# Windowed attention and a squared-ReLU layer on one core: loads without a gate from tile 9 on, scores of tiles 12 on two steps sooner

## The chip, the cores and the metric

The kernel runs on one core of a Trainium2 chip. A core has five engines that work side by side, each through its own list of instructions in order: TensorE multiplies matrices (in the profile PE, and PEld for its loading of weights), VectorE (DVE) and ScalarE (ACT) work on elements, GpSimd (POOL) here only starts loads, and SyncE (SP) starts the other DMA transfers. All transfers run on the core's 16 DMA engines. An engine waits for another through semaphores, and a transfer tells by a semaphore that it has landed. The metric is the device time of the program in microseconds (us); less is better.

## The reference

The inputs are q, k and v of 4 batches, 8 heads, 768 positions and 64 values per head, and the weights w_in (512 x 2048) and w_out (2048 x 512), all float32. First comes attention, in which a position sees the first 8 positions of its batch and the 96 positions up to itself, with a bias that falls with the distance by a slope of its own for each head; then, for each of the 3072 rows of 512 values, a layer with a squared ReLU:

```python
scores = scale * np.matmul(q, k.transpose(0, 1, 3, 2))
is_global = pos[None, :] < int(n_global)            # 8
is_local = (rel >= 0) & (rel < int(n_local))        # 96
keep = is_global | is_local
dist = np.where(is_global & ~is_local, float(n_local), np.abs(rel).astype(np.float32))
scores = scores + -slopes[:, None, None] * dist
scores = np.where(keep, scores, -1000000000.0)
a = softmax(scores)                                 # over the last axis
attn = np.matmul(a, v)
x = attn.transpose(0, 2, 1, 3).reshape(B * S, H * D)
h = x @ w_in
r = np.maximum(h, 0.0)
out = (r * r) @ w_out
```

## The kernel before

**Tiles and blocks.** The 3072 rows are 24 *tiles* of 128 positions, six per batch; two tiles are a *block* of the layer, so there are 12 blocks. Since the window is 96 long, a tile's queries need the keys of their own tile and of the one before; the 8 global keys are copied into that one's place.

**What happens to a tile j.** (1) *Load*: POOL starts three transfers, q, k and v (`load_tile`, the DMA at L200), which change float32 to bfloat16 on the way. q and k go into a slot of the ring `qk_ring`; tiles from 6 on share three slots, so tile j takes the slot of tile j - 3. v has a buffer for each tile. (2) *Turn*: the values of a head must lie along the partitions for the products. For the first six tiles TensorE transposes q and k; from tile 6 on one DMA transposition, started by SP (L407, `qkT<-qk`), does it. I call it the turn of tile j. When it has landed, the slot is free. (3) *Scores*: 16 small products per tile on TensorE (L463, `sc<-qkT`), 8 for the first tile of a batch. (4) ScalarE takes the exponential (L509, `esc<-sc`), VectorE multiplies it by a table of the bias and the mask (L534, `at<-esc`). (5) *Values*: TensorE multiplies with v in two halves of four heads (L576, `po<-v,at`), VectorE divides by the sum (L603, L604), which gives the tile's x. (6) *Move of x*: from tile 6 on a second DMA transposition on SP (L663, `xT<-x`) turns x for the layer.

**What happens to a block.** For each of eight steps s, TensorE makes an *up group*, eight products of 256 columns with w_in (L689, `hT<-xT,win`); ScalarE takes the ReLU (L710), VectorE squares it (L722, `hs<-hr`), and TensorE makes two *down pairs*, two products of 512 columns each with w_out (L759, `acc<-wout,hs`), one for each tile of the block. After the eighth step ScalarE or VectorE copies each tile's sum (L315, L317, `o<-acc`), and SP stores it (L794).

**What sets the order.** The order is not written out by hand. The program describes each piece of work as an operation with its engine, a cost, the operations that it needs and a due time, the *key*; the class `Plan` then goes through them, always taking the operation with the least start plus a hundredth of its key, and the result is the order of instructions on each engine. The key of a tile's work comes from its *base*, counted in steps of the layer, eight to a block:

```python
need = 8 * (j // 2)
base = need - LEADS.get(j, LEAD) + 4 * (j % 2)      # LEAD = 12
```

`LEADS` is a table of exceptions. Besides, scores of tile j may not be planned ahead of a certain up group (end of `order1`), which uses LEAD alone.

**The gate.** A load is issued by POOL in program order. For tiles from 8 on the plan puts an operation ahead of it, the *gate*: VectorE writes zeros into one column of the slot (L357). The load overwrites it, so POOL has to wait until VectorE has come to that place in its own list. The gate needs the end of the slot's last turn, the data of the tile before, and comes after the move of x of tile j - 3 was issued. Its `emit` is:

```python
nc.vector.memset(qk_ring[slot(j)][:, :, :1], 0.0)
```

**The queues.** POOL's list is loads alone, in the order of tiles after the start-up. SP's list holds turns, moves of x and stores, in the plan's order; each waits at the head of the queue for its own data, and what stands behind it waits with it. In the kernel before, SP's list runs, with the tile's number: turn 8, x 7, turn 9, x 8, two stores, turn 10, x 9, turn 11, x 10, two stores, turn 12, x 11, turn 13, x 12, two stores, turn 14, and so on.

Of the kernel before, what the change touches and what calls it, by code (L numbers as in the profile page):

```python
# [104 lines left out]
def kernel(  # L105
# [17 lines left out]
    NT = B * TPB  # L123
# [17 lines left out]
    NFIRST = 4  # L141
# [3 lines left out]
    NQ, NKT = 3, 2 * TPB  # L145
# [29 lines left out]
    pbt = const([P, 2, P], FP32, "pbt")  # L175
    pbw = const([P, 2, P], FP32, "pbw")
    plan = Plan()
    LEADS = {6: 10, 7: 11}
    NHS = 14
    NWARM = 8  # L180
    NLATE, NO = 2, 4
# [9 lines left out]
    def slot(j):  # L191

        return j if j < NFIRST + 2 else NFIRST + 2 + j % NQ
# [34 lines left out]
    def load_tile(j):  # L228
        load_part(0, j)
        load_part(1, j)  # L230
        load_v(j)
# [111 lines left out]
    for j in range(NT):  # L343
        b, t = divmod(j, TPB)
        first = t == 0
        need = 8 * (j // 2)
        base = need - LEADS.get(j, LEAD) + 4 * (j % 2)


        if j in late:  # L350
            def emit_load(e, j=j):
                load_tile(j)
            gate = None
            if j >= NFIRST + 2 + NQ - 1:

                def emit_gate(e, j=j):
                    nc.vector.memset(qk_ring[slot(j)][:, :, :1], 0.0)  # L357

                gate = plan.op(
                    ("gate", j), {"DVE": 0.07}, emit_gate, deps=qk_users[slot(j)] + [ld, xT_sp.get(j - 3)],  # L360
                    key=base - 9,
                )
            ld = plan.op(
                ("load", j), {"POOLQ": 2.6}, emit_load,
                deps=qk_users[slot(j)] + [ones[j], gate], key=base, ready=issue[0],
            )
            qk_users[slot(j)] = []
            ld = plan.op(("data", j), {"DMAQ": 2.7}, None, deps=[ld])
            land["q", j] = land["k", j] = land["v", j] = ld
# [360 lines left out]
    for o in plan.ops:  # L730
        if o["name"][0] == "sc":
            j = o["name"][1]
# [113 lines left out]
```

## Time and profile before

| | |
|---|---|
| time, median of 4 runs | 213.78 us (213.58 to 214.06) |
| time of the profiled execution | 214.06 us |
| its span, first to last instruction | 212.3 us |
| TensorE busy | 205.0 us, 97% of the span, at full granted clock |
| VectorE, ScalarE, POOL busy | 139.7, 119.9, 73.8 us |
| loads: q, k, v, from issue to landing, median | 4.6, 5.1, 5.7 us |
| turns (x18) and moves of x (x18), from issue to landing, median | 3.5 and 3.6 us |
| stores, from issue to landing, median | 2.2 us |

The profile is of one execution. Its times count from the start of the span. A line of the timeline gives start, length, engine, source line, operation, what is written from what, how many in a row, and in brackets how long the engine was idle before, and what ended that. A line of the chain of work gives start, length and what; the chain goes back from the last instruction, at each step to what released it. A line of the waits gives who waited at which line for whom, the sum in us, how often, and the longest. A transfer's line on POOL or SP shows its issue alone; when it landed is a separate figure. The products of TensorE are pipelined, so their lengths overlap; the step from one start to the next tells the pace.

### The profile page before, as it was taken

Reading aid. Unit: us, or ns where it says so; the run is one execution under the profiler, and the core shown is the slowest. Engines: PE = TensorE matmul, PEld = TensorE weight load, DVE = VectorE, ACT = ScalarE, POOL = GpSimd, SP = SyncE. Lnnn points to the kernel's source line nnn. Section 1 sums busy time; section 2 is a strip of 40 time slices with the busy share of each in tenths; the row PEclk is TensorE's granted clock in tenths of the full one; section 3 lists DMA queues with packets and bytes.
Section 4 is the critical chain, followed back from the end, with each engine's and each line's share of the span. In section 5 each row is a group of like instructions: output and inputs, shape, how many; then the busy total and the mean of one; then the engine's idle time right before and its main releaser. Section 6 shows DMA issues by size and latency. Waiting matters only on the chain.

```text
span 212.3 us, 5014 instructions
## 1 busy us (share of the span) xinstructions
PE 205.0 (97%) x1976; PEld 141.2 (67%) x1976; DVE 139.7 (66%) x377; ACT 119.9 (56%) x223; POOL 73.8 (35%) x91
## 2 busy tenths in 40 slices
PE   7999999999999999989989999999999999999994
PEld 3778777656766767757656767666767667666773
DVE  7789878524876966755757677575677587464530
ACT  6897478215664573753845854753845754743531
POOL 8998665440404413404404404314134310000000
PEclk9999999999999999999999999999999999999999
DMA  9999999999799999799999699998999894210202
GB/s 133 148 176 185 185 192 199 172 190 140 180 105 119 182 114 124 141 150 87 153 130 101 107 182 93 119 185 96 164 141 99 115 183 80 88 36 3 99 2 99
DMA packets 113703, 27.59 MB, mean 130 GB/s; under 512 B 104336, under 2 KB 110736, under 8 KB 113680
## 3 DMA queue, kind: packets, MB, share of 16 engines
q0 software_dynamic: 79200, 13.37, 82.6%
q1 hardware_dynamic: 34480, 13.90, 33.2%
q8 instruction: 15, 0.25, 0.5%
q14 instruction: 8, 0.07, 0.1%
HBM read 27.26 MB, written 6.29 MB: 158 GB/s over the span
## 4 chain that ended last, share of the span: by engine, by line
PE 78%; DMA 10%; POOL 7%; ACT 1%; issue 1%; SPq 0%; POOLq 0%; ACTq 0%
PE acc L759 36%; PE hT L689 33%; DMA qkT<-qk 6%; PE sc L463 5%; DMA win<-in_moe_w_in_dram 4%; POOL qk L200 4%; PE po L576 4%; POOL v L200 2%; POOL win L200 1%; ACT o L315 1%; ACT esc L509 1%; SPq L794 0%; POOL wout L200 0%; PE trx L639 0%; ACT hr L710 0%
## 5 line engine op out<-in xcount | busy, mean ns | idle before, releaser
L759 PE MATMUL acc<-wout,hs 128*128 128x512 bf16 (+1 forms) x400 | 99.0, 371 | 0.0
L689 PE MATMUL hT<-xT,win 128*128 128x256 bf16 x768 | 98.3, 273 | 0.6 <-DMA win<-in_moe_w_in_dram 0.4
L710 ACT ACTIVATE hr<-hT 128x512 f32<-128x512 f32 x96 | 57.7, 601 | 72.5 <-PE hT L689 69.5
L689 PEld LDWEIGHTS <-win 128*128 128x128 bf16 x768 | 73.9, 98 | 25.7 <-DMA win<-in_moe_w_in_dram 1.6
L722 DVE TENSOR_TENSOR hs<-hr 128x512 bf16<-128x512 f32 x96 | 65.7, 688 | 32.5 <-ACT hr L710 31.4
L200 POOL DMA_DIRECT2D qk<-in_q_dram x23 | 20.6, 896 | 90.2 <-DVE qk L357 56.1
L759 PEld LDWEIGHTS <-hs 128*128 128x128 bf16 x400 | 35.7, 98 | 23.7
L509 ACT ACTIVATE esc<-sc 128x512 bf16<-128x512 f32 x78 | 43.6, 608 | 5.1 <-PE sc L463 5.1
L534 DVE TENSOR_TENSOR at<-esc,E 128x512 bf16<-128x512 bf16 x78 | 32.2, 422 | 11.2 <-ACT esc L509 9.9
L200 POOL DMA_DIRECT2D v<-in_v_dram x24 | 21.7, 904 | 1.4 <-DMA win<-in_moe_w_in_dram 1.0
L604 DVE TENSOR_TENSOR x<-po,rs 128x256 bf16<-128x256 f32 x48 | 20.4, 425 | 1.7
L200 POOL DMA_DIRECT2D qk<-in_k_dram x23 | 20.5, 899 | 0.5 <-DMA win<-in_moe_w_in_dram 0.5
L576 PEld LDWEIGHTS <-at 128*128 128x128 bf16 x352 | 16.1, 98 | 4.6 <-ACT at L509 0.8
L576 PE MATMUL po<-v,at 128*128 128x65 bf16 x352 | 17.8, 193 | 0.5 <-ACT at L509 0.3
L463 PEld LDWEIGHTS <-qkT 64*128 64x128 bf16 x352 | 10.0, 94 | 9.0 <-DMA qkT<-qk 4.3
L315 ACT COPY o<-acc 128x512 f32<-128x512 f32 (+1 forms) x21 | 11.2, 568 | 7.6 <-PE acc L759 7.6
L463 PE MATMUL sc<-qkT 64*128 64x128 bf16 x192 | 13.2, 219 | 1.7 <-DMA qkT<-qk 1.6
L603 DVE RECIPROCAL rs<-po 128x4 f32<-128x4 f32 x48 | 8.6, 180 | 9.1 <-PE po L576 8.8
L463 PE MATMUL sc<-qkT,qkT 64*128 64x128 bf16 x160 | 11.4, 216 | 0.0
L200 POOL DMA_DIRECT2D wout<-in_moe_w_out_dram x8 | 5.7, 718 | 2.8 <-DMA win<-in_moe_w_in_dram 2.0
L200 POOL DMA_DIRECT2D win<-in_moe_w_in_dram x8 | 6.2, 800 | 1.1 <-DMA win<-in_moe_w_in_dram 0.4
L550 DVE COPY qkT<-qkT 128x32 bf16<-128x32 bf16 x16 | 2.8, 174 | 5.6 <-PE sc L463 5.6
(41 smaller groups left out, 59.3 us busy)
## 6 DMA issues: line engine op xcount, KB each, us to landing
out_dram<-o SPq DMA_DIRECT2D x23, 256.0 KB, 2.2
v<-in_v_dram POOLq DMA_DIRECT2D x24, 128.0 KB, 5.7
qk<-in_q_dram POOLq DMA_DIRECT2D x23, 128.0 KB, 4.6
qk<-in_k_dram POOLq DMA_DIRECT2D x23, 128.0 KB, 5.1
win<-in_moe_w_in_dram POOLq DMA_DIRECT2D x8, 256.0 KB, 8.0
wout<-in_moe_w_out_dram POOLq DMA_DIRECT2D x8, 256.0 KB, 9.5
qkT<-qk SPq DMA_TRANSPOSE x18, 3.5
xT<-x SPq DMA_TRANSPOSE x18, 3.6
```

Of the source, the lines that this page charges most:

```text
L200: nc.gpsimd.dma_start(out=dst, in_=src)
L315: nc.scalar.copy(dst, src)
L463: nc.tensor.matmul(out=tiles["sc", j, odd, g][:, at, :], lhsT=qkT[(j - kt) % NKT][half, 1, pair, :], rhs=qkT[j % NKT][half, 0, pair, :], s ...
L509: nc.scalar.activation(out=esc, in_=tiles.pop(("sc", j, odd, g)).rearrange("p a c -> p (a c)"), func=Act.Exp, scale=scale,)
L534: nc.vector.tensor_mul(at, tiles.pop(("esc", j, odd, g)), bias)
L576: nc.tensor.matmul(out=po[:, hi, :], lhsT=tiles["at", j, odd, g][:, at * P : (at + 1) * P], rhs=v_sb[kj][:, h, :], start=(i == 0), stop=(i ...
L603: nc.vector.reciprocal(rs, po[:, :, D : D + 1])
L604: nc.vector.tensor_tensor(out=x[:, 4 * hf : 4 * hf + 4, :], in0=po[:, :, :D], in1=rs.to_broadcast([P, 4, D]), op=Alu.mult,)
L689: nc.tensor.matmul(out=hT[:, c, :], lhsT=w_in_sb[s][:, kt, c * P : (c + 1) * P], rhs=tiles["xT", blk][:, kt, :], start=(kt == 0), stop=(kt ...
L710: nc.scalar.activation(hr, tiles.pop(("hT", blk, s)), Act.Relu)
L722: nc.vector.tensor_mul(hs, hr, hr)
L759: nc.tensor.matmul(out=tiles["acc", blk, sub, half], lhsT=hs[:, c, sub * P : (sub + 1) * P], rhs=w_out_sb[s][:, c, cols], start=(s == 0 an ...
```

## The change

From tile 9 on there is no gate: the load of a tile needs the end of the turn that last read its slot, and its turn in POOL's list. The gate of tile 8 stays. And for tiles 12 to 23 the lead in the table is 14 in place of 12, so that every key of these tiles' work (load, turn, scores, exponentials, values, move of x) is two steps lower.

```diff
     plan = Plan()
-    LEADS = {6: 10, 7: 11}
+    LEADS = {6: 10, 7: 11} | {j: 14 for j in range(12, NT)}
+    JGATE = 9
     NHS = 14
...
             def emit_load(e, j=j):
                 load_tile(j)
             gate = None
-            if j >= NFIRST + 2 + NQ - 1:
+            if NFIRST + 2 + NQ - 1 <= j < JGATE:
 
                 def emit_gate(e, j=j):
                     nc.vector.memset(qk_ring[slot(j)][:, :, :1], 0.0)
```

NFIRST + 2 + NQ - 1 is 8, NT is 24. No product, no exponential and no transfer is added or taken away. Since the plan decides with other keys and other needs, the order changes on TensorE, VectorE, ScalarE and SP; POOL's list stays as it is. SP's list now runs: turn 8, turn 9, x 7, turn 10, x 8, two stores, turn 11, x 9, turn 12, x 10, two stores, turn 13, x 11, x 12, turn 14, turn 15, x 13, two stores, turn 16, and so on.

## The prediction

> **What bounds the kernel now.** I read the page first, then the chain that ended last, then TensorE's timeline where it is idle, then the queues of SP and POOL there. The page:
>
> ```profile
> span 212.3 us, 5014 instructions
> PE 205.0 (97%) x1976; PEld 141.2 (67%) x1976; DVE 139.7 (66%) x377; ACT 119.9 (56%) x223; POOL 73.8 (35%) x91
> ```
>
> TensorE is the bound. From 25.6 us on the groups on it follow without holes: eight up products (x8 of 128x256) take 0.87 us, four down products (128x512) 0.86 us, a tile's sixteen score products 0.55 us plus 0.1 us of entry, one half of its value products 0.24 us. The change adds and removes no product, so it can win only idle time of TensorE. The list of waits by window shows where that is after the start-up: two places, both before scores.
>
> ```profile
> 91.94 0.59 PE L759 MATMUL acc<-wout,hs 128*128 128x512 bf16 x2
> 93.22 0.40 PE L463 MATMUL sc<-qkT 64*128 64x128 bf16 x8 [0.69 <-DMA qkT<-qk]
> ...
> 108.42 0.59 PE L759 MATMUL acc<-wout,hs 128*128 128x512 bf16 x2
> 109.96 0.23 PE L463 MATMUL sc<-qkT 64*128 64x128 bf16 x2 [0.95 <-DMA qkT<-qk]
> ```
>
> These are the scores of tiles 12 and 14, and they wait for the tile's *turn*, the DMA transposition qkT<-qk at L407: 0.69 + 0.95 = 1.64 us. The chain of work says why the turn of tile 12 was late:
>
> ```profile
> 85.62 0.60 ACT o L315
> ...
> 86.24 0.33 SPq L794
> ...
> 86.68 6.50 DMA qkT<-qk
> ...
> 93.22 0.40 PE sc L463 x8
> ```
>
> ScalarE's copy of an output tile releases its store (L794), and the turn stands behind that store in SP's queue. It then takes 6.50 us instead of the 3.0 us of a turn with nothing beside it (93.33), because the load of tile 13 began at 86.32. Tile 14 repeats it at 103.25 with 6.67 us.
>
> What starts a load is seen in POOL's waits and timeline:
>
> ```profile
> POOL qk L200 <- DVE qk L357: 56.1, 11, 7.1
> ...
> 44.79 0.88 POOL L200 DMA_DIRECT2D qk<-in_q_dram  x1 [4.95 <-DVE qk L357]
> ...
> 56.20 0.89 POOL L200 DMA_DIRECT2D qk<-in_q_dram  x1 [8.78 <-DVE rs L603]
> ...
> DMA to landing us min/median/max: 3.0/3.5/6.8
> ```
>
> The first line is the gate, a memset of 60 ns on VectorE (L357, x16) that each load waits for. The two below are the loads of tiles 8 and 9. The last line, of the turns alone, is the price list that I use: 3.0 us with nothing beside it, 6.5 to 6.8 us behind a load.
>
> [...] So a turn behind a load is told finished about when that load is; the trace agrees (turn of tile 12 lands at 93.18, the k part of load 13, issued at 87.19, at about 93.3). [...] the trace's groups give 0.87/8 = 109 and 0.43/2 = 215 ns. [...]
>
> **The change, part by part.**
>
> *Gates of tiles 9 to 23 go.* 15 memsets of 60 ns, 0.9 us of VectorE, which is 66% busy and on no wait of TensorE there: worth 0. If that cover were gone it would be 0.06 us each.
>
> *Loads start earlier.* A load now waits only for the turn that read its slot last and for POOL's own order. Turn 6 was issued at 43.47 and landed 5.2 us later, at 48.7; so load 9 starts at 48.7 instead of 56.20. Turn 7 (45.43 + 6.8) gives 52.2 for load 10 instead of 63.75. Each has three parts at 0.87 to 0.90 us, so load 10 ends its issue at about 54.9. Later loads follow in the same way, some 8 to 15 us ahead of before.
>
> *Turns move on SP's queue.* In the built order turn 9 stands ahead of the move of x of tile 7 (L663), not behind it, turn 10 ahead of x 8, turn 12 ahead of x 10 and of the store pair that held it; turn 14 comes right after x 12. Each turn issues one DMA of 1.2 to 1.3 us of SP, and SP has room (SP's waits in the window 80 to 112 sum to over 25 of 32 us).
>
> *Scores of tiles 12 on move.* Counted in the built order, the scores of tile 12 have two up groups, five down pairs and one value half fewer ahead of them: 2 x 0.87 + 5 x 0.43 + 0.24 = 4.1 us sooner; tile 14: 3.9 us; tiles 13 and 15: 3.5 us. A turn has to be ready that much sooner. Tiles 9 to 11 come 0.9 to 1.3 us sooner, tile 8 one down pair (0.43 us) later.
>
> *Are the two holes closed?* Tile 12, without its stall, was due at 92.5; now 88.4. Its turn can go when x 9 is issued (74.14 + 2.05 = 76.2); behind a load at the worst 6.8 us, so 83: 5 us to spare. Tile 14 was due at 108.2 (first hole taken out), now 104.3. Its turn follows x 12, issued at 97.56 before and about 4 us sooner now, so 94.8 + 6.8 = 101.6: 2.7 us to spare. Tile 13 now stands behind a store pair, about 87.2 + 6.8 = 94 against scores due at 100.4 - 0.7 - 3.5 = 96.2. So 1.64 us are won.
>
> *Where it is paid back.* Turn 8 keeps its place and time (54.99, behind x 6), but what surrounds it is new: before, load 9 started after it, at 56.20, and it took 3.1 us (landing at 58.1, scores at 60.04, 1.9 us to spare). Now load 10 ends its issue just ahead of it, with load 9 before that. The scores of tile 8 are due at 60.04 + 0.43 = 60.5. No row of before shows a turn behind two loads. Low end: 3.1 us, no wait. High end: 6.8 us plus the three further parts of load 9 at 0.85 us each (the parts of load 7, issued at 37.21 and 38.08, both took 7.3 us, so land 0.87 us apart): 9.4 us, landing at 64.4, a stall of 3.9 us. For the value I take the closest pattern, a transposition issued 1.0 us after the last part of a load: x 9 at 74.14, 5.6 us. A turn alone takes 3.0 us and an x alone 2.4 us, so 5.6 + 0.6 = 6.2 us: landing at 61.2, a stall of 0.7 us. Turn 7 lands at 52.2, 0.15 us ahead of its scores at 52.38, with load 9 now issued beside it: 0 to 0.3 us, I take 0. The first up group of block 3 began at 64.81, just after x 7 landed (58.65 + 6.0 = 64.7), and stands 0.7 us later now; x 7 has turn 9 ahead of it in place of load 9: 0 to 0.5 us, I take 0.
>
> *Sum.* On the profiled execution: 214.06 - 1.64 + 0.7 = 213.1 us, in span 212.3 - 0.9 = 211.4 us. Its time is 0.28 us over the median of the runs, 213.78. On the median: 213.78 - 0.94 = **212.8 us**. The floor, both holes closed and nothing paid back, is 212.1 us, or 212.0 if the holes are counted from start to start of the products.
>
> **Rivals.**
>
> *Slower: turn 8 drowns.* It sits behind loads 9 and 10 and lands as the high end says. Each microsecond past 60.5 costs one microsecond. It decides where the stall is over 1.64 + 0.43 us, that is where the turn takes more than 7.6 us. At 9.4 us: 213.78 - 1.64 + 3.9 = 216.0 us; midway, at 8.5 us, 215.1. For it: two loads back to back, which before never put ahead of a turn. Against it: load 9 starts 3.5 us ahead of load 10 and should be nearly through, and no transposition took over 6.8 us. About 215.
>
> *No change: the wait moves.* The stalls leave tiles 12 and 14 and come back elsewhere, at tile 13 behind its store pair, at x 9 before the up groups of block 4, or at tile 8 with 1.2 to 2 us. For it: loads in bursts of two or three, x 9 and x 12 already taking 5.6 and 6.4 us beside a load. Against it: the margins above, 2 us and more. About 213.7.
>
> *It doesn't do what it says.* Loads go early, but the turns still wait behind the stores, and the holes stay: 213.8. The built order speaks against it: turns 12 and 14 no longer follow a store directly.
>
> **How the numbers follow.** Forecast (212.0 to 213.3): 0.66. No change, by the last two rivals: 0.15. Slower: 0.19. Under 0.2% (0.43 us) a measurement of this kernel can't be told from no change, since its four runs spread over 0.48 us; so faster 0.66, same 0.15, slower 0.19. The range runs from 211.9, the floor less 0.1 of scatter, to 214.6, which leaves out the upper half of the slower case, about 0.13, and some hundredths below. The likeliest case's own range is 212.0 to 213.3.
>
> **What would show it.** Right: no wait of TensorE on qkT between 80 and 112 us; q of load 9 issued near 48.7 and of load 10 near 52.2; turn 8 landing 5 to 7 us after its issue, with an idle of TensorE before the scores of tile 8, near 60.5, under 1.3 us; all later turns landing 2 us or more ahead of their scores. Wrong: turn 8 over 7.6 us; idle before scores of other tiles or before the first up group of a block; gaps of TensorE released by VectorE or ScalarE, whose order I have taken as harmless.

## The result: 0.24% slower in this series, where 0.5% faster was predicted

The changed kernel takes 214.22 us (median of 43 runs, 213.28 to 216.91) against 214.02 us (64 runs, 212.35 to 217.94) for the kernel before. The ratio is 1.0024, with a 95% interval of 1.0008 to 1.0041. The forecast was 212.8 us, faster. Single executions of either kernel differ by up to 5.6 us; the ratios leave the disturbed ones out, and so do the medians given with the experiments below, but a ratio is not simply that of two medians.

The profiled execution took 214.14 us. Its page:

```profile
span 212.4 us, 4979 instructions
PE 204.8 (96%) x1976; PEld 140.7 (66%) x1976; DVE 141.3 (67%) x366; ACT 116.8 (55%) x219; POOL 73.8 (35%) x91
```

TensorE does the same 1976 products in the same time (204.8 us, 205.0 before). The two holes before the scores of tiles 12 and 14 are gone: in TensorE's waits (who waited, at which line, for whom; sum, times, longest) only one is left on a turn in the whole execution.

```profile
PE sc L464 <- DMA qkT<-qk: 1.1, 1, 1.1
```

TensorE's timeline puts it at tile 8, where the kernel before had 1.9 us to spare:

```profile
60.16 1.03 PE L760 MATMUL acc<-wout,hs 128*128 128x512 bf16 x4
62.27 0.23 PE L464 MATMUL sc<-qkT 64*128 64x128 bf16 x2 [1.08 <-DMA qkT<-qk]
```

The brackets count idle time from the modelled end of the last product. Counted from start to start, less the usual step between products and the 0.1 us of entry that all scores have, it is 1.15 us; holes and stalls are given in that count from here on. The chain of work shows what it hangs on:

```profile
54.19 0.89 PE hT L690 x8
55.08 1.09 SPq L664
...
56.27 5.96 DMA qkT<-qk
62.23 0.04 issue
62.27 0.62 PE sc L464 x16
```

Turn 8 starts at 56.27, late behind the move of x of tile 6 (L664), and takes 5.96 us. In the kernel before it started at 54.99 and took 3.1 us. What stands ahead of it is seen in the timelines of POOL and SP:

```profile
49.55 0.89 POOL L201 DMA_DIRECT2D qk<-in_q_dram  x1 [1.48 <-DMA qkT<-qk]
...
52.63 0.88 POOL L201 DMA_DIRECT2D qk<-in_q_dram  x1 [0.44 <-issue]
53.50 0.88 POOL L201 DMA_DIRECT2D qk<-in_k_dram  x1
54.37 0.90 POOL L201 DMA_DIRECT2D v<-in_v_dram  x1
```

```profile
53.18 0.90 SPq L795 DMA_DIRECT2D out_dram<-o  x2
54.31 1.85 SPq L664 DMA_TRANSPOSE xT<-x  x1
56.27 4.70 SPq L408 DMA_TRANSPOSE qkT<-qk  x2
```

Load 9 starts at 49.55, load 10 at 52.63, and inside load 10 come two stores and the move of x of tile 6. All of them stand in front of turn 8. The stores and the move stood there in the kernel before too (52.53 and 53.66); the two loads are new. So one stall at tile 8 has come in place of two holes at tiles 12 and 14. The experiments had to say whether load 10 is its cause, whether the stall is as large as the holes, and what the holes were worth.

**Theory A**: load 10 ahead of turn 8 makes that turn late, and the stall pays the gain back. **Theory B**: the earlier scores, or the order on TensorE in general, cost the time, and the stall is a detail of one execution.

### The profile page after: what moved, and what is told of

It reads as the page before. It is cut to its first block, busy times and chain, and to the rows that moved or that the text cites. A ratio compares the mean times of both kernels' runs of the same rounds, so it can differ in the third digit from the quotient of the medians.

```text
span 212.4 us, 4979 instructions
## 1 busy us (share of the span) xinstructions
PE 204.8 (96%) x1976; PEld 140.7 (66%) x1976; DVE 141.3 (67%) x366; ACT 116.8 (55%) x219; POOL 73.8 (35%) x91
## 3 DMA queue, kind: packets, MB, share of 16 engines
HBM read 27.26 MB, written 6.29 MB: 158 GB/s over the span
## 4 chain that ended last, share of the span: by engine, by line
PE 85%; DMA 7%; POOL 5%; SPq 1%; issue 0%; ACT 0%; POOLq 0%
PE acc L760 38%; PE hT L690 37%; PE sc L464 5%; PE po L577 4%; DMA win<-in_moe_w_in_dram 4%; DMA qkT<-qk 3%; POOL qk L201 3%; POOL v L201 2%; POOL win L201 1%; SPq L664 1%; PE tr L384 0%; PE trx L640 0%; ACT o L316 0%; POOL pbi L255 0%; SPq L408 0%
## 5 line engine op out<-in xcount | busy, mean ns | idle before, releaser
L510 ACT ACTIVATE esc<-sc 128x512 bf16<-128x512 f32 x78 | 41.5, 608 | 3.0 <-PE sc L464 2.9
L316 ACT COPY o<-acc 128x512 f32<-128x512 f32 (+1 forms) x17 | 9.3, 561 | 10.0 <-PE acc L760 9.5
L551 DVE COPY qkT<-qkT 128x32 bf16<-128x32 bf16 x16 | 3.4, 210 | 9.3 <-PE sc L464 9.2
L318 DVE COPY o<-acc 128x512 f32<-128x512 f32 x8 | 5.5, 692 | 2.5 <-PE acc L760 2.4
```

The lines of the kernel that those rows point to most:

```text
L316: nc.scalar.copy(dst, src)
L510: nc.scalar.activation(out=esc, in_=tiles.pop(("sc", j, odd, g)).rearrange("p a c -> p (a c)"), func=Act.Exp, scale=scale,)
```

## The experiments

**The changed kernel again**, without an edit, since one execution shows one stall.

> The changed kernel once more. Theory A (turn 8 pays): the scores of tile 8 wait 1.0 to 2.5 us for turn 8, which is issued near 55 to 56 us and takes 5.5 to 7.5 us; no other wait on qkT; ratio to the kernel before 1.000 to 1.004. Theory B (the start-up differs, not the turns): the first scores after the start-up again begin some 0.6 us later than before, and the wait at tile 8 is under 0.8 us.

Measured: 214.41 us (21 runs) against 214.82 (35 runs of the kernel before), ratio 0.9968 (0.9944 to 0.9991). This series has it a little ahead, where the first had it a little behind, and outside the 1.000 to 1.004 that Theory A was given. The waits of TensorE in its profiled execution:

```profile
PE sc L464 <- DMA qkT<-qk: 1.8, 1, 1.8
```

Again one wait, again at tile 8, but turn 8 took 7.32 us, not 5.96, and the stall is 1.87 us. The stall is there again, and its size is no constant.

**The gates of tiles 9 and 10 kept**, so that neither load stands ahead of turn 8. All else as in the changed kernel, planned anew:

```diff
-    JGATE = 9
+    JGATE = 11
```

> The change with the gates of tiles 9 and 10 kept (the gates end at tile 11). Theory A: no load stands ahead of turn 8, which takes 3.0 to 3.5 us; no wait of TensorE on qkT from 40 us on; the whole of the two holes of before is won: 1.6 us, ratio 0.9925 (0.990 to 0.995). Theory B: the ratio stays within 0.998 to 1.004, since the start-up keeps its loss. Theory C (the holes of before are small in most runs): ratio 0.996 to 0.998.

Measured: 215.76 us (14 runs), ratio 1.0048 (1.0018 to 1.0078). Theory A's first half came true and its number, 0.9925, did not. Turn 8 took 3.09 us and nothing waits for it, but the stall has moved to tile 10, and grown:

```profile
68.64 1.08 ACT o L316 x2
...
69.73 0.33 SPq L795
...
70.17 9.45 DMA qkT<-qk
79.61 0.05 issue
79.66 1.03 PE sc L464 x16
```

Load 11 is now the first without a gate. In the new plan it goes ahead of load 10, which still waits for its gate (59.09 against 64.03), so POOL's order changed too. Behind them load 12 stands ahead of turn 10 as load 10 stood ahead of turn 8: its parts are issued from 68.29 to 70.92, the two stores at 69.24 and 69.73, the turn at 70.17. The last part of load 12 (v, issued 70.02) took 9.59 us and landed at 79.61, at the same time as the turn. The hole is 3.10 us long, and the clock granted to TensorE after it is 0.50 for a while; that is taken up at the end. This execution took 218.44 us, among the longest of the 22 (213.91 to 218.49), so its sizes are not typical ones. Keeping two gates moved the burst and its stall to the place where the gates now end.

**Gates alone** taken away, the scores of tile 12 on where they were:

```diff
-    LEADS = {6: 10, 7: 11} | {j: 14 for j in range(12, NT)}
+    LEADS = {6: 10, 7: 11}
     JGATE = 9
```

> The first half alone: no gate from tile 9 on, leads as before. Theory A: turn 8 is behind loads 9 and 10 as in the changed kernel, the wait at tile 8 is 1.0 to 2.5 us, the holes at tiles 12 and 14 are gone, since their turns no longer follow a store pair and a load: ratio 1.000 to 1.004, as the changed kernel. If the earlier scores cost something of their own, this one is faster than the changed kernel by over 0.2%.

Measured: 214.64 us (18 runs), ratio 0.9992 (0.9963 to 1.0020). Turn 8 took 6.29 us, with a stall of 1.12 us. The scores did move a little with the gates gone, but those of tile 12 have one up group fewer ahead of them than in the kernel before, not two as in the changed kernel: the early scores that Theory B names aren't needed for the stall. The waits of TensorE show a second one:

```profile
PE hT L690 <- DMA xT<-x: 1.2, 1, 1.2
...
PE sc L464 <- DMA qkT<-qk: 1.1, 1, 1.1
```

The move of x of tile 15, issued at 122.56 just behind the v part of a load (122.43), landed with it at 129.84, and block 7 waited.

**Leads alone**, with all gates kept:

```diff
-    LEADS = {6: 10, 7: 11}
+    LEADS = {6: 10, 7: 11} | {j: 14 for j in range(12, NT)}
     JGATE = NT
```

> The second half alone: leads of 14 from tile 12 on, all gates kept. Theory A: turn 8 takes about 3.1 us and no wait at tile 8; scores and turns of tiles 12 on both move two steps, the turns still behind store pairs and loads, so holes of 0.5 to 3 us in all at tiles 12 on: ratio 0.997 to 1.006. If the leads are what costs, ratio over 1.004 with waits at tiles 12 on.

Measured: 217.88 us (4 runs), ratio 1.0134 (1.0078 to 1.0191). This is the worst of all, and it is what was written down for the case that the leads are what costs. The waits of TensorE, in an execution of 220.12 us (the six ran from 216.28 to 220.36):

```profile
PE sc L464 <- DMA qkT<-qk: 5.5, 4, 2.4
```

Holes stand before the scores of tiles 7 (0.52 us), 12 (0.71), 14 (2.46) and 20 (2.05). But the run doesn't test early scores. With the gates kept, the plan left the scores where they were: the trace has 312 up products ahead of the scores of tile 12 and 376 ahead of tile 14, as in the kernel before, and only tile 18 differs, by one up group more. What moved is work in between (value products, ReLUs, squares, one store) and gates. Turn 14, again behind a store pair, took 7.66 us in place of 6.67, and turn 20, now just behind the first part of load 21, took 7.79 us in place of 3.35. Why the whole came out that much slower wasn't taken apart. So the second part of the change loses when it stands alone, and the first part alone does as well as both.

**Load 10 alone held back.** The changed kernel's plan and order; only load 10 is emitted later, behind a memset on VectorE of one column of its slot (as the gate does), placed after the division that ends x of tile 7. Since POOL's list is in order, loads 11 and on follow it (in the profile 10 starts at 58.17, 11 at 60.76 and 12 at 63.36).

```diff
     for o in plan.run({"PE": 4.2, "DVE": 4.2, "ACT": 5.3, "DMAQ": issue[1]}):
-        if o["emit"]:
+        if o["name"] == ("load", 10):
+            held = o
+        elif o["emit"]:
             o["emit"](o["engine"])
+            if o["name"] == ("norm", 7, 1):
+                nc.vector.memset(qk_ring[slot(10)][:, :, :1], 0.0)
+                held["emit"]("POOLQ")
```

> The changed kernel, with one thing moved: load 10 waits for a memset that VectorE reaches right after it has divided the second half of tile 7 (near 58.5 us), so that it starts behind turn 8 and not ahead of it; the order of all else is that of the changed kernel. Theory A (load 10 ahead of turn 8 is what costs): turn 8 takes 3.0 to 4.5 us, no wait of over 0.3 us before the scores of tile 8, and the time is 1.2 to 2.0 us less than that of the changed kernel. Rival (load 9 alone, or the move of x ahead of turn 8, makes it late; or the time goes elsewhere): turn 8 still takes 5.5 us or more, or the time stays within 0.5 us of the changed kernel's.

Measured: 212.45 us (6 runs, 212.11 to 213.06) against 214.19 (29 runs of the kernel before), ratio 0.9889 (0.9852 to 0.9926). It is 2.2 us less than the changed kernel in the same series (214.63, below). Its POOL timeline and, after it, TensorE's at the scores of tile 8:

```profile
49.52 0.89 POOL L201 DMA_DIRECT2D qk<-in_q_dram  x1 [2.55 <-DMA qkT<-qk]
50.39 0.89 POOL L201 DMA_DIRECT2D qk<-in_k_dram  x1
51.25 0.90 POOL L201 DMA_DIRECT2D v<-in_v_dram  x1
58.17 0.88 POOL L201 DMA_DIRECT2D qk<-in_q_dram  x1 [6.01 <-DVE v L622]
```

```profile
59.44 1.03 PE L760 MATMUL acc<-wout,hs 128*128 128x512 bf16 x4
60.40 0.23 PE L464 MATMUL sc<-qkT 64*128 64x128 bf16 x2
```

Load 9 starts at 49.5 as in the changed kernel, load 10 only at 58.17, after turn 8; the memset that it waits for ran at 57.80, beside the copy that the bracket names. Turn 8, issued at 54.97, took 3.72 us and landed 1.7 us ahead of its scores, which start at 60.40 without idle before them. The two stores and the move of x still stand ahead of the turn (52.46 and 53.59), and so does load 9; together they make it 0.6 us longer than in the kernel before, which costs nothing. This settles Theory A: load 10 ahead of turn 8 is what costs, and with load 10 out of the way the rest of the change is worth 1.1% by the ratio, 0.8% by the medians. It settles Theory B as well, since the order on TensorE is that of the changed kernel, early scores and all.

**The kernel before, turns ahead of stores.** To price the two holes in plain runs, the kernel before with one edit of SP's order alone: the store pairs of blocks 3 to 8 are held back until the turn behind them (tiles 12, 14, ... 22) has been emitted.

```diff
+    held, gone = [], set()
...
         if o["emit"]:
+            if o["name"][0] == "st" and 3 <= o["name"][1] <= 8 and ("T", 2 * o["name"][1] + 6) not in gone:
+                held.append(o)
+                continue
             o["emit"](o["engine"])
+            if o["name"][0] == "T" and len(o["name"]) == 2:
+                gone.add(o["name"])
+                for h in held:
+                    h["emit"](h["engine"])
+                held.clear()
```

> The kernel before, with the even turns 12 to 22 put ahead of the store pair that stands before them on SP's queue; all else as before. It prices the holes of the kernel before. If they are 1.64 us in a plain run as in the profiled one: ratio to the kernel before 0.992 (0.990 to 0.994), turns 12 and 14 land over 1 us ahead of their scores. If a plain run has smaller holes: 0.995 to 0.999. If the store pair is not what makes these turns late: the waits before the scores of tiles 12 and 14 stay.

Measured: 212.39 us (6 runs, 212.13 to 213.66), ratio 0.9890 (0.9850 to 0.9930). SP's timeline:

```profile
84.30 1.23 SPq L407 DMA_TRANSPOSE qkT<-qk  x1
85.70 1.35 SPq L794 DMA_DIRECT2D out_dram<-o  x2
...
100.50 1.23 SPq L407 DMA_TRANSPOSE qkT<-qk  x1
101.82 1.51 SPq L794 DMA_DIRECT2D out_dram<-o  x2
```

The turns of tiles 12 and 14 go 1.4 and 1.3 us ahead of the stores, take 3.72 and 3.96 us, and no product waits for them; two waits of 0.2 us are left, at tiles 6 and 7. With gates and leads as they were, this is as fast as the version with load 10 held. The two holes were worth 1.8 us by the medians of this series (214.19 less 212.39); by the interval of the ratio, 1.5 to 3.2 us.

**Both kernels once more**, without an edit, beside those two.

> The changed kernel beside the two above on the same chip. Theory A: turn 8 takes 5.5 to 7.5 us, the scores of tile 8 wait 1.0 to 2.2 us, no wait on qkT later; it stands between the kernel before and the version that holds load 10: ratio to the kernel before 0.996 to 1.003.

Measured: 214.63 us (21 runs), ratio 1.0021 (0.9997 to 1.0045). Turn 8 took 7.58 us, and the stall is 1.85 us; tile 7 had a stall of 0.29 us.

```profile
61.40:63.30 1.90, 0.15 (x1) 0.00 (x0) 0.65 (x1) 0.00 (x0) 0.00 (x0) 1.00 1.69 180
```

In this window of TensorE's hole (length; busy time of TensorE, its loads, VectorE, ScalarE, POOL; granted clock; DMA share; GB/s) TensorE is busy for 0.15 us and VectorE for 0.65 us, the others not at all: the core waits for a transfer.

> The kernel before once more, for a second trace of its holes. If the holes are the same in every execution: 0.7 and 1.0 us before the scores of tiles 12 and 14, none elsewhere. If they come and go (turns 12, 14, 16, 18, 20 and 22 landed 0.0 to 0.3 us ahead of their scores, but for turn 20 with 2.5): other sizes, at other even tiles, 0 to 4 us in all.

Measured: 214.37 us (15 runs), ratio of before to itself 0.9996 (0.9963 to 1.0029).

```profile
PE sc L463 <- DMA qkT<-qk: 1.9, 2, 1.0
```

Its two holes are where they were, at tiles 12 and 14, of 0.93 and 1.06 us. In the first profile of it they were 0.75 and 1.02 us.

**Where the spans go.** The two versions without these stalls (load 10 held, turns ahead of stores) have a span of 210.5 us each, and the other spans follow from it. "Due" is when the scores of tile 8 would have started without their stall; it is 60.40 in the version with load 10 held.

| profiled execution | over 210.5 | made up of |
|---|---|---|
| before | 1.8 | holes 0.75 + 1.02 |
| before again | 2.1 | holes 0.93 + 1.06 |
| after | 1.9 | due at 61.12, so 0.72 late; stall 1.15 |
| after again | 2.1 | due at 60.66, so 0.26 late; stall 1.87 |
| after, third | 3.0 | due at 61.48, so 1.08 late (0.29 of it at tile 7); stall 1.85 |

In every row the parts give the span to about 0.1 us. The lateness outside tile 7 comes from the start-up: all of it is seen already at the scores of tile 6 (49.75, 49.28 and 49.82 us in the three executions of after, 49.03 with load 10 held, whose order is the same up to there), before the first load without a gate has landed. That it is scatter, and not something of the change, isn't shown. What the change takes from one place, some 1.8 to 2.0 us, it puts down in another, 1.1 to 1.9 us and now and then some tenths more.

**Why turn 8 takes what it takes.** Landings, read from each transfer's issue and length:

| execution | v of load 10: issued + length = lands | turn 8: issued + length = lands |
|---|---|---|
| after | 54.37 + 7.03 = 61.40 | 56.27 + 5.96 = 62.23 |
| after again | 54.69 + 7.52 = 62.21 | 55.17 + 7.32 = 62.48 |
| after, third | 55.60 + 7.68 = 63.28 | 55.70 + 7.58 = 63.28 |
| gates alone | 54.23 + 6.41 = 60.63 | 55.08 + 6.29 = 61.36 |

In all four the turn lands 0.0 to 0.8 us after the last part of the load in front of it, and its own issue time decides little: issued 1.1 us later (56.27 against 55.17), it lands at nearly the same time (62.23 against 62.48). What ties the two landings together isn't shown.

## Why the prediction was wrong

*The bound and the place of the gain* were right. TensorE's products cost the same, both holes closed, and in the profile of after no turn from tile 9 on came close to its scores (the closest, turn 14, landed at 100.97, 5.0 us ahead of them). The order on SP and the starts of loads were right too: load 9 at 49.55 and load 10 at 52.63 against 48.7 and 52.2, in an execution whose turn 6 was issued 0.65 us later than before.

*The floor* was right to 0.5 us. It was put at 212.0 to 212.1 us; the versions without these stalls run at 212.39 and 212.45, in a series in which the kernel before takes 214.19 and not 213.78.

*The size of the gain*, 1.64 us from the list of waits, was a little small: 1.77 and 1.99 us from start to start in two executions, and 1.8 us by the medians. This error alone would have made the forecast too slow.

*The step that failed is "Where it is paid back".* It put the scores of tile 8 due at 60.5, which the version with load 10 held shows to be right (60.40), and turn 8 at 6.2 us, landing at 61.2, a stall of 0.7 us. Measured: 5.96, 7.32 and 7.58 us, landings at 62.23, 62.48 and 63.28, and stalls of 1.15, 1.87 and 1.85 us. The pattern that I took, the move of x of tile 9 behind one load, has no second load, no stores and no other transposition between. The turn should have been priced by the load in front of it, since the prediction had itself read that a turn behind a load lands about when that load does. (The row it gave for that does not show it: the k part of load 13 was issued 0.5 us after turn 12. The table above does.) The prediction had the number at hand: the parts of load 7 took 7.3 us. The v part of load 10, issued near 54.0 by its working, would have landed at 61.3, the turn 0 to 0.8 us later, with a stall of 0.8 to 1.6 us. That the first of the three lengths lies near 6.2 us is luck: that turn was issued 1.3 us later than forecast. It also took turn 8 to "keep its place and time (54.99)"; it keeps its place, but the move of x ahead of it took 1.85 us of SP in the profile of after instead of about 1.2, and the turn went at 56.27.

*The rivals.* "The wait moves" gave tile 8 with 1.2 to 2 us as one of its forms, and about 213.7 us. That is what happened, within the scatter; I had it at 0.15, together with the rival that the change doesn't do what it says. "Turn 8 drowns" names the right mechanism at too high a price: the turn never passed its point of decision of 7.6 us. The reason I gave against it, that load 9 should be nearly through, is true (load 9 costs nothing), but load 10 was enough.

*What stays open.* Whether the changed kernel is really slower. The three series gave 1.0024, 0.9968 and 1.0021, the first and second with intervals on opposite sides of 1. Each kernel carries 1.2 to 2.1 us of stalls, whose length differs by execution, so their difference is one of two scattering numbers. Why the leads alone lose as much as they do is open too. Which of the transfers beside load 10 (two stores, a move of x) makes its last part take 6.4 to 7.7 us wasn't taken apart.

## What to carry to other kernels

Price a transfer that gates the critical engine by the landing of what was issued just ahead of it (here 0.0 to 0.8 us before its own, in four executions), under the load of everything in flight there, and not by its own usual duration. Taking a throttle off a prefetch freed a burst where the throttle ended, both times that it was tried here (stalls of 1.1 to 1.9 us at tile 8, 3.10 us at tile 10), so look at the first few users there. Holding back one load by 5 us, or in the kernel before putting six store pairs each behind a turn, gave about 212.4 us, about 1% under the kernel before, while the change as it stood gave nothing. Check also that an edit moved what it was meant to move: the leads alone moved no score forward. A stall read from one profile is a sample; take two or three before setting it against a gain of the same size.

## What was not expected of the hardware

*Two long holes were followed by half the clock.* After the 3.10 us hole at tile 10 in the run with gates 9 and 10 kept, TensorE was granted half the clock (windows as above; the clock is the third number from the end):

```profile
76.40:79.60 3.20, 0.23 (x2) 0.00 (x0) 0.69 (x1) 0.43 (x1) 0.00 (x0) 0.86 1.51 116
79.60:81.00 1.40, 1.34 (x17) 0.90 (x18) 0.25 (x2) 0.70 (x2) 0.54 (x1) 0.50 1.28 286
81.00:83.50 2.50, 2.37 (x10) 1.52 (x10) 1.20 (x3) 0.97 (x3) 2.50 (x4) 0.50 0.94 66
83.50:85.50 2.00, 1.91 (x12) 1.05 (x12) 0.69 (x1) 0.99 (x2) 2.00 (x3) 0.50 1.52 97
85.50:90.00 4.50, 4.50 (x51) 3.04 (x49) 2.50 (x8) 1.26 (x3) 2.84 (x4) 1.00 2.28 145
```

And after the 2.46 us hole at tile 14 in the run with the leads alone, beside its hole of 2.05 us at tile 20:

```profile
109.70:112.20 2.50, 0.18 (x1) 0.00 (x0) 0.69 (x1) 0.38 (x1) 0.00 (x0) 1.00 1.80 138
112.20:115.50 3.30, 2.89 (x24) 2.12 (x26) 1.89 (x6) 2.06 (x4) 0.71 (x1) 0.51 0.43 81
...
161.80:164.00 2.20, 0.22 (x2) 0.00 (x1) 0.69 (x1) 0.42 (x1) 0.00 (x0) 1.00 2.27 167
164.00:168.00 4.00, 3.95 (x45) 2.81 (x47) 2.68 (x9) 2.56 (x5) 1.70 (x2) 1.00 0.56 100
```

At half clock the eight up products from 81.45 on run for 1.91 us; at full clock such a group runs for 1.04 us (from 108.41 in the second run). The trace has the clock down from 78.71 to 85.53 in the first, 6.82 us, and from 112.27 to 115.69 in the second, 3.42 us. By the brackets of idle time, the clock fell 2.1 us into the first hole (3.03 us) and at the end of the second (2.40 us), while it stayed at 1.00 through 1.80 and 1.78 us before the scores of tile 8 in the second and third executions of after, and through 1.98 us at tile 20. What decides whether it falls, and for how long, isn't shown. By half the time at half clock, an estimate, the first hole cost some 2.9 us more (from 79.66 to 85.53), nearly its own length again, the second 1.7 us.

The profiled execution with the second stretch has a mean clock of 0.992, the one with the first 0.984. In the last series 9 of the 61 plain executions of the kernel before have a mean clock of 0.990 to 0.992, and 6 of the 22 of the changed kernel, but none of the 12 of the two versions without these stalls. So some executions of both kernels may pay for their stalls twice; no trace of one was kept, and it isn't shown.

*Transpositions in a crowd.* The prediction leaned on "no transposition took over 6.8 us". That held in both executions of the kernel before, at 6.80 and 6.81 us, and not beyond them: turn 7 took 7.65 us in the version with turns ahead of stores, whose order up to there is that of the kernel before; turn 10 took 9.45 us above; and turn 16 took 9.82 us in the profile of after, hidden there because it still landed 6.6 us ahead of its scores.
